# A spectral-mix kernel: six late weight steps become three, and half of their products become 48 small SBUF-to-SBUF transfers

## The chip, the cores and the metric

One core of one Trainium2 chip. The metric is device time in microseconds; the kernel before has a median of 180.15 us over 3 runs (179.83 to 180.81). The engines are called TensorE (matrix products, PE in the profile, its weight loads PEld), VectorE (DVE), ScalarE (ACT), GpSimd (POOL) and SyncE (SP). GpSimd and SyncE issue the transfers.

## The reference

`x` has 8 batches, 3264 positions and 192 channels. Two stages follow each other:

```python
w = softmax(weight)                        # 8 heads x 7 taps
x = causal_conv(x, w)                      # per head of 24 channels
X = rfft(x, axis=1)[:, :64]                # 64 modes, per batch and channel
Yr = Xr @ w_r - Xi @ w_i                   # per mode, 192 x 192
Yi = Xr @ w_i + Xi @ w_r
y = irfft(Y, n=3264)
u = x + y
out = u + maximum(u @ w_ch, 0)
```

All is linear up to the maximum, so `u @ w_ch` is computed as `x @ w_ch` plus the inverse transform of `Y @ w_ch`, and the output of a tile of 128 positions is the clamped sum of two products, plus the inverse transform of `Y`, plus `x`.

## The kernel before, in words

**Loads and convolution (to about 53 us).** GpSimd's queue loads `x` in units (L142) into `xall`, converted to bf16. TensorE convolves with banded matrices in `band` (L270), VectorE and ScalarE copy the result back over `xall` (L279, L277), and products with the cosine and sine table `ftab` (L288) give the spectrum, which `xtrans` lays out as `xt`, in the tile `mixa`.

**Mode products (about 68 to 108 us).** `mix(g, bank)` (L407) takes the 64 modes in 16 groups of four. The weights of a group are two transfers of 288 KB on GpSimd's queue (L251), 16 groups in all. The result of a group is a PSUM block whose partition is 32 x (mode within the group) + 8 x (real or imaginary) + batch; `mix_copy` (L420) copies it to `ymix`, two buffers used in turn. `mix_trans` (L424) transposes it on TensorE, and VectorE and ScalarE sort it into `yet` (L435, L437), with the channel as partition and batch, real or imaginary part and mode as columns. Between groups, transposes of `xall` into `ct` fill the time (`c_bank`, L381). For the last four groups that filling is used up, and `warm` (L533, its products are L536) puts filler products between: 12, 3, 5, 2 and 13.

**First weights.** For a batch `b`, `zw_mm` (L478) multiplies `yet` with `wm` and `w1`, which hold `w_ch` in columns 0 to 191 and an identity in columns 192 to 383. So one bank gets `Y @ w_ch` (used as "g") and `Y` back with modes as partitions ("y"), each 192 columns. `zw_out` (L482) scales it by `ascale` (1/S for mode 0, 2/S for the others) and writes it to `zw`, which lies over `xt` in `mixa`. Batches 0 and 1 are done ahead of the loop (L567 to L571).

**The output loop (about 109 to 174 us).** Two batches form a pair `q` (four pairs); two neighbouring tiles of positions form a duo (13 for each pair, 52 in all). Duos 0 and 1 are written out by hand with whole 128-row products (`full`, L522; `whole`, L573). The other 100 items, `(duo, a)` from duo 2 on, run through the loop at L635. TensorE works on the upper and lower 64 rows at once: for item k the lower rows' c and g products, for item k-2 the upper ones (L595), then a clamp by ScalarE (L514), then the y products of items k-4 and k-5. VectorE adds `x` to the bank (L501) and SyncE sends a duo out (L509). Eight PSUM banks go round in a ring (`next_of_ring`, L586), and seven output buffers in `arena`.

The order is written out by hand. `WEIGHTS` (L608) says after which loop steps the weights of batches 2 to 7 are made: six steps (9, 19, 29, 39, 51, 63), each with two products of 384 columns (L479, L480), a bank of the ring and a ScalarE scaling (L487). Pair 1 is first used by the g product of item 22 and by the y product of that item four steps later; pair 2 by item 48, pair 3 by item 74. Transfers on GpSimd's queue use eight completion counters in turn: a transfer waits for the one that was issued eight before it.

Of the kernel before, what the change touches and what calls it, by code (L numbers as in the profile page):

```python
# [9 lines left out]
ALU = mybir.AluOpType  # L10
ACT = mybir.ActivationFunctionType
AX = mybir.AxisListType
F32 = mybir.dt.float32
BF16 = mybir.dt.bfloat16
# [5 lines left out]
def kernel(  # L20
# [9 lines left out]
    nc = tc.nc  # L30
    B, S, D = x.shape
    H, KK = weight.shape
    MODES = moe_w_r.shape[0]
# [3 lines left out]
    P = 128  # L37
# [17 lines left out]
    def sb(name, shape, dtype):  # L55
        return pool.tile([P] + shape, dtype, tag=name, name=name)
# [8 lines left out]
    yet = sb("yet", [2, B, 2 * MODES], BF16)  # L65
    mixa = sb("mixa", [3 * 2 * B * MODES], BF16)
    xt = mixa[:, :].rearrange("p (j k m) -> p j k m", j=3, k=2 * B)
    zw = mixa[:, 0:2 * B * D].rearrange("p (t b d) -> p t b d", t=2, b=B)
    band = sb("band", [H, 2 * P], BF16)
    wm = sb("wm", [2 * D], BF16)  # L70
    w1 = sb("w1", [2 * D], BF16)
    wsw = sb("wsw", [2 * D], BF16)
# [2 lines left out]
    ascale = sb("ascale", [1], F32)  # L75
    halfpi = sb("halfpi", [1], F32)
    xs = [sb(f"xs{i}", [2, D], BF16) for i in range(2)]
    ymix = [sb(f"ymix{i}", [2, D], BF16) for i in range(2)]

    late = ct[:, 3 * NT * (NQ - 1):3 * NT * NQ, :].rearrange("p t s -> p (t s)")  # L80
    spots = [arena[:, WGB * i:WGB * (i + 1)] for i in range(NW)]
# [9 lines left out]
    def temp(n, dtype):  # L91
        w = n * 2 if dtype == F32 else n
        a = arena[:, pos[0]:pos[0] + w]
        pos[0] += (w + 15) // 16 * 16
        return a.bitcast(dtype) if dtype != BF16 else a

    turns = temp(NT * MODES, F32)
    whole = temp(NT * MODES, F32)
# [63 lines left out]
    nc.vector.memset(xall[HALF:P, NT:NSLOT:NT, :, :], 0.0)  # L162
    nc.vector.memset(halfpi[:], math.pi / 2)
    nc.vector.memset(ascale[:], 2.0 / S)
    nc.vector.memset(ascale[0:1, :], 1.0 / S)
    nc.vector.memset(ascale[64:65, :], 1.0 / S)
    for _ in range(NIDLE):
        nc.tensor.matmul(ZC[2][:, 0, 0:2 * D], xall[:, 0, 0, 0:P], xall[:, 0, :, :], start=True, stop=True,
                         skip_group_check=True)
    nc.vector.tensor_scalar(out=cidx[:, 0:PW], in0=cidx[:, 0:PW], scalar1=goff[:, 0:1], scalar2=None, op0=ALU.add)  # L170
    for k in range(KK):
        nc.vector.tensor_scalar(out=masks[:, PW * k:PW * (k + 1)], in0=cidx[:, 0:PW],
                                scalar1=float(KK - 1 - k), scalar2=None, op0=ALU.is_equal)
# [16 lines left out]
    for g in range(4):  # L190
        dst, srcv = band[32 * g:32 * g + 32, :, 32 * g:32 * g + PW], pk3[32 * g:32 * g + 32, :, :]
# [162 lines left out]
    ze, zm = [z[:, 0, :] for z in z4[0:2]], [z[:, 0, :] for z in z4[2:4]]  # L354
# [17 lines left out]
    def trans(o, in_):  # L372
        nc.tensor.matmul(o, in_, ident[:], start=True, stop=True, is_transpose=True)  # L373
# [33 lines left out]
    def mix(g, bank):  # L407
        yp = bank[:, D * (g % 2):D * (g % 2) + D]
        for j in range(3):
            for p4 in range(4):  # L410
                m = 4 * g + p4
                nc.tensor.matmul(yp[32 * p4:32 * p4 + 2 * B, :], xt[:, j, :, m],  # L412
                                 wts[g][:, p4, j, :], start=(j == 0), stop=(j == 2),
                                 tile_position=(0, 32 * p4), skip_group_check=True)
        if g < NW:
            load_w(g + NW + 3)
        elif g >= NW + 3:
            load_w(g + NW)

    def mix_copy(d, bank, g0, n):  # L420
        nc.scalar.copy(out=ymix[d % 2][:, g0:g0 + n, :],  # L421
                       in_=bank[:, D * g0:D * (g0 + n)].rearrange("p (g d) -> p g d", g=n))

    def mix_trans(d, g0, n):  # L424
        et = [z.bitcast(BF16)[:, 0:n * P].rearrange("p (g k) -> p g k", g=n) for z in ze]
        for t in range(2):
            for g in range(n):
                trans(et[t][:, g, :], ymix[d % 2][:, g0 + g, 64 * t:64 * t + P])
        m0 = 8 * d + 4 * g0
        for t in range(2):  # L430
            dst = yet[:, t, :, :].rearrange("p b (c m) -> p c b m", c=2)[:, :, :, m0:m0 + 4 * n]
            srcv = et[t].rearrange("p g (q k) -> p (g q) k", q=4)[:, :, 0:16].rearrange(
                "p m (c b) -> p c b m", c=2)
            if t == 0:
                nc.vector.tensor_copy(out=dst, in_=srcv)  # L435
            else:
                nc.scalar.copy(out=dst, in_=srcv)  # L437
# [15 lines left out]
    def turn(names):  # L453
        nop = nc.tensor.nop()
        for name in names:
            tc.add_manual_dep(nop.ins, name, mybir.DependencyInfo(mybir.DependencyClass.Sync,
                                                                  mybir.DependencyReason.DATA),
                              reason="row tiles take turns on a bank")
# [16 lines left out]
                last[row] = mm.ins.name  # L475
        held[n] = (first, last)

    def zw_mm(b, bank):  # L478
        nc.tensor.matmul(bank[:, 0:2 * D], yet[:, 0, b, :], wm[:], start=True, stop=False)  # L479
        nc.tensor.matmul(bank[:, 0:2 * D], yet[:, 1, b, :], w1[:], start=False, stop=True)  # L480

    def zw_out(b, bank, on_scalar, t=None):  # L482
        ts = slice(0, 2) if t is None else slice(t, t + 1)
        dst = zw[:, ts, b, :]
        srcv = bank[:, 0:2 * D].rearrange("p (t d) -> p t d", t=2)[:, ts, :]
        if on_scalar:
            nc.scalar.activation(out=dst, in_=srcv, func=ACT.Copy, scale=ascale[:, 0:1])  # L487
        else:
            nc.vector.tensor_scalar(out=dst, in0=srcv, scalar1=ascale[:, 0:1], scalar2=None, op0=ALU.mult)

    duos = [((q, 2 * b), (q, 2 * b + 1)) for q in range(NQ) for b in range(NB)]
    N = len(duos)
    place = {}
# [17 lines left out]
    def clamp(bank, on_scalar=True):  # L511
        z = bank[:, 0:2 * D]
        if on_scalar:
            nc.scalar.activation(out=z, in_=z, func=ACT.Relu)  # L514
        else:
            nc.vector.tensor_scalar(out=z, in0=z, scalar1=0.0, scalar2=None, op0=ALU.max)
# [5 lines left out]
    def full(n, which, a):  # L522
        (q, t), _ = duos[n]
        nc.tensor.matmul(place[n][a][:, 0:2 * D], ftab[:, t + a, :],  # L524
                         zw[:, 0 if which == "g" else 1, 2 * q:2 * q + 2, :].rearrange("p b d -> p (b d)"),
                         start=False, stop=(which == "y"), skip_group_check=True)
# [6 lines left out]
    def warm(bank, n):  # L533

        for _ in range(n):
            nc.tensor.matmul(bank[:, 0:2 * D], xall[:, 0, 0, 0:P], xall[:, 0, :, :], start=True, stop=True,  # L536
                             skip_group_check=True)
# [11 lines left out]
    c_products(1)  # L549
    d = ND - 2  # L550
    mix(2 * d, zm[0])
    warm(zm[1], 12)
    mix(2 * d + 1, zm[0])
    mix_copy(d, zm[0], 0, 2)
    warm(zm[1], 3)
    mix_trans(d, 0, 2)
    warm(zm[1], 5)
    d = ND - 1
# [1 line left out]
    mix_copy(d, zm[1], 0, 1)  # L560
    warm(zm[0], 2)
    mix_trans(d, 0, 1)
    warm(zm[0], 13)
    mix(NG - 1, zm[0])
    mix_copy(d, zm[0], 1, 1)
    mix_trans(d, 1, 1)
    zw_mm(0, zm[0])  # L567
    zw_mm(1, zm[1])
    for t in range(2):
        zw_out(0, zm[0], False, t)  # L570
        zw_out(1, zm[1], True, t)  # L571

    def whole(n, which):  # L573
        for a in range(2):
            full(n, which, a)
# [10 lines left out]
    def next_of_ring():  # L586
        taken[0] += 1
        return ring[(taken[0] - 1) % 8]

    bank = {}  # L590
    end = {}

    def product(k, row, piece, first, last):
        cols, l, r = piece
        mm = nc.tensor.matmul(bank[k][:, cols], l, r, start=first, stop=last, skip_group_check=True)  # L595
        end[k, row] = mm.ins.name

    def pieces(k, row, which):
        if not 0 <= k < K:
            return []  # L600
        n, a = items[k]
        return [p for w in which for p in z_pieces(duos[n][a], row, w)]

    def take(k):
        bank[k] = next_of_ring()
        place.setdefault(items[k][0], []).append(bank[k])

    WEIGHTS = {9: 2, 19: 3, 29: 4, 39: 5, 51: 6, 63: 7}  # L608

    def upper_y(k):  # L610
        if 0 <= k < K - 2:
            turn([end[k, 0]])
            product(k, 1, pieces(k, 1, "y")[0], False, True)
            add(bank[k], *items[k])
# [10 lines left out]
    for k in range(LAG):  # L625
        take(k)
        for j, p in enumerate(pieces(k, 0, "c")):
            product(k, 0, p, j == 0, False)
    whole(0, "g")
    clamp(place[0][0], False)  # L630
    clamp(place[0][1])
    whole(1, "g")
    clamp(place[1][0], False)
    clamp(place[1][1])
    for k in range(K + 4):  # L635
        if LAG <= k < K:
            take(k)
        lower, upper = pieces(k, 0, "cg"), pieces(k - LAG, 1, "cg")
        if upper:
            turn([end[k - LAG, 0]])  # L640
        for j in range(4):
            if j == 2:
                upper_y(k - 5)
            if j == 3:
                lower_y(k - 4)
            if lower and (k >= LAG or j == 3):
                product(k, 0, lower[j], j == 0, False)
            if upper:
                product(k - LAG, 1, upper[j], False, False)
        if upper:  # L650
            clamp(bank[k - LAG])
        if k in WEIGHTS:
            z = next_of_ring()
            zw_mm(WEIGHTS[k], z)
            zw_out(WEIGHTS[k], z, True)
        if k in (1, 2):
            whole(k - 1, "y")
            for a in range(2):
                add(place[k - 1][a], k - 1, a)
# [32 lines left out]
```

## Time and profile before

| | |
|---|---|
| median of 3 runs | 180.15 us (179.83 to 180.81) |
| profiled execution | 180.46 us |
| its span in the profile | 178.0 us |
| busy: PE, DVE, ACT, POOL | 164.2, 120.2, 107.9, 49.5 us |
| L595, all products of the loop: 64x384 / 64x192 | 57.0 us (396) / 84.6 us (600) |
| L501, adds by VectorE | 57.1 us (104), 557 ns each |
| L514, clamps by ScalarE | 48.4 us (102), 475 ns each |
| L487, scalings by ScalarE in the loop | 575 ns each (6) |
| L509, transfers out | 54, 3.1 us to landing (median) |
| L251, weight transfers on GpSimd's queue | 32, 612 ns each to issue, 11.5 us to landing |

The span is what the profiler recorded between the first and the last instruction; the executions' times hold some microseconds more. A row of a view names an engine, a line of the kernel and an operation. "Idle before" is how long the engine had nothing to run, and the arrow names what ended that. The chain that ended last goes back from the last instruction to whatever released it, and prints it in order of time: start, length, what. Products of TensorE are pipelined, so one product's duration (323 ns for 384 columns) is longer than the distance between two (160 ns).

### The profile page before, as it was taken

How to read it: one execution, taken by the hardware profiler on the slowest of the kernel's cores; microseconds unless marked ns; L12 is line 12 of the kernel's file. 1: busy time of each engine (PE TensorE's matmuls, PEld its weight loads, DVE VectorE, ACT ScalarE, POOL GpSimd, SP SyncE). 2: the span in 40 equal slices, each digit the busy share in tenths (PEclk: the TensorE clock that was granted, in tenths of full speed). 3: DMA queues.
4: the chain of work that ended last, by engine and by line, in shares of the span. 5: the costliest groups of instructions: out<-in, count | busy, mean ns of one | idle time of the engine just before them, and what ended most of it. 6: DMA issues, size and time to landing. Idle time of an engine off the chain costs nothing.

```text
span 178.0 us, 6536 instructions
## 1 busy us (share of the span) xinstructions
PE 164.2 (92%) x2773; PEld 136.6 (77%) x2773; DVE 120.2 (68%) x224; ACT 107.9 (61%) x193; POOL 49.5 (28%) x78
## 2 busy tenths in 40 slices
PE   7977999999999988999697988999999999999990
PEld 3557989999899976899695543877787887899960
DVE  6669874365354644788764004888988988999991
ACT  6347784344534424877474114688788888888870
POOL 7998931555233244443442000000000000000000
PEclk9999999999999999999999999999999999999998
DMA  4999999999999999999999940588888979899996
GB/s 47 160 187 192 194 190 192 193 190 192 193 192 195 207 207 206 206 206 206 206 207 206 206 71 4 182 301 312 290 317 308 340 277 344 304 337 330 332 357 211
DMA packets 50029, 40.04 MB, mean 225 GB/s; under 512 B 28304, under 2 KB 50000, under 8 KB 50000
## 3 DMA queue, kind: packets, MB, share of 16 engines
q0 software_dynamic: 35488, 19.54, 79.3%
q1 hardware_dynamic: 14512, 20.09, 30.8%
q8 instruction: 21, 0.34, 0.8%
q14 instruction: 8, 0.07, 0.1%
HBM read 39.10 MB, written 20.05 MB: 332 GB/s over the span
## 4 chain that ended last, share of the span: by engine, by line
PE 54%; DMA 33%; POOL 6%; issue 2%; ACT 1%; DVE 0%; DVEq 0%; POOLq 0%
PE z L595 33%; DMA arena<-in_moe_w_i_dram 20%; PE z L270 10%; DMA ct<-in_moe_w_i_dram 6%; DMA xall<-in_x_dram 6%; PE z L288 5%; POOL xall L142 4%; PE z L536 1%; PE z L479 1%; PE z L524 1%; PE z L480 1%; POOL xall L230 1%; PE z L412 0%; ACT xall L277 0%; POOL arena L251 0%
## 5 line engine op out<-in xcount | busy, mean ns | idle before, releaser
L501 DVE TENSOR_TENSOR arena<-z,xall 128x384 f32<-128x384 f32 (+1 forms) x104 | 57.1, 557 | 6.1 <-PE z L595 4.0
L595 PE MATMUL z<-mixa,ftab 64*128 64x384 bf16 x396 | 57.0, 323 | 0.0
L514 ACT ACTIVATE z<-z 128x384 f32<-128x384 f32 x102 | 48.4, 475 | 11.8 <-PE z L595 3.0
L595 PEld LDWEIGHTS <-ct 64*128 64x128 bf16 x600 | 37.8, 94 | 8.1 <-PE z L595 1.9
L270 PE MATMUL z<-xall,band 128*64 128x192 bf16 (+3 forms) x832 | 39.0, 246 | 2.3 <-ACT band L193 1.1
L270 PEld LDWEIGHTS <-band 128*64 128x64 bf16 x832 | 36.3, 110 | 4.5 <-issue 2.3
L279 DVE CAST xall<-z 128x768 bf16<-128x768 f32 (+3 forms) x26 | 24.8, 956 | 22.0 <-PE z L270 19.6
L595 PE MATMUL z<-wsw,ct 64*128 64x192 bf16 x300 | 33.4, 242 | 0.0
L595 PEld LDWEIGHTS <-ftab 64*128 64x128 bf16 x396 | 32.2, 94 | 1.1 <-issue 0.3
L277 ACT CAST xall<-z 128x768 bf16<-128x768 f32 (+3 forms) x26 | 20.7, 798 | 20.1 <-PE z L270 19.9
L142 POOL DMA_DIRECT2D xall<-in_x_dram x26 | 23.6, 914 | 12.1 <-DMA xall<-in_x_dram 11.3
L595 PE MATMUL z<-wm,ct 64*128 64x192 bf16 x200 | 26.9, 244 | 0.0
L595 PE MATMUL z<-w,ct 64*128 64x192 bf16 x100 | 24.3, 243 | 0.0
L365 DVE COPY ct<-z 128x1024 bf16<-128x1024 bf16 x26 | 17.1, 687 | 7.7 <-PE z L373 4.8
L288 PE MATMUL z<-xall,ftab 128*64 128x384 bf16 (+1 forms) x208 | 21.0, 326 | 0.7 <-ACT xall L277 0.7
L373 PE MATMUL z<-ident,xall 128*128 128x128 bf16 x312 | 19.3, 219 | 0.2 <-ACT ftab L363 0.2
L373 PEld LDWEIGHTS <-xall 128*128 128x128 bf16 x312 | 17.7, 98 | 1.0 <-issue 0.3
L363 ACT COPY ct<-z 128x1024 bf16<-128x1024 bf16 x13 | 13.2, 1013 | 4.0 <-PE z L373 3.9
L288 PEld LDWEIGHTS <-ftab 128*64 128x64 bf16 (+1 forms) x208 | 13.5, 110 | 2.3 <-DVE xall L279 0.5
L251 POOL DMA_DIRECT2D arena<-in_moe_w_r_dram x13 | 8.0, 614 | 15.3 <-PE z L373 5.3
L421 ACT CAST ymix<-z 128x384 bf16<-128x384 f32 (+1 forms) x9 | 4.0, 444 | 13.1 <-PE z L412 13.0
L251 POOL DMA_DIRECT2D arena<-in_moe_w_i_dram x13 | 8.0, 613 | 11.3 <-DMA xall<-in_x_dram 5.5
(95 smaller groups left out, 122.5 us busy)
## 6 DMA issues: line engine op xcount, KB each, us to landing
out_dram<-arena SPq DMA_DIRECT2D x47, 384.0 KB, 3.2
xall<-in_x_dram POOLq DMA_DIRECT2D x14, 384.0 KB, 13.4
arena<-in_moe_w_r_dram POOLq DMA_DIRECT2D x13, 288.0 KB, 11.6
arena<-in_moe_w_i_dram POOLq DMA_DIRECT2D x13, 288.0 KB, 11.8
xall<-in_x_dram POOLq DMA_DIRECT2D x6, 432.0 KB, 13.8
ct<-in_moe_w_r_dram POOLq DMA_DIRECT2D x3, 288.0 KB, 11.2
ct<-in_moe_w_i_dram POOLq DMA_DIRECT2D x3, 288.0 KB, 11.2
out_dram<-arena SPq DMA_DIRECT2D x3, 288.0 KB, 3.4
```

The lines of the kernel that those rows point to most:

```text
L142: nc.gpsimd.dma_start(out=xall[:, s0:s0 + nf, i, :], in_=src)
L251: nc.gpsimd.dma_start(out=wts[g][64 * half:64 * half + 64, :, :, :], in_=src[4 * g:4 * g + 4, :, :].rearrange("m (p j) e -> p m j e", j=3))
L270: nc.tensor.matmul(o, lhs, xall[:, r0:r0 + 2 * n - 1:2, :, dsl], start=(main and a == 0), stop=not main, tile_position=(0, 64 * half), ski ...
L277: nc.scalar.copy(out=dst, in_=srcv)
L279: nc.vector.tensor_copy(out=dst, in_=srcv)
L288: nc.tensor.matmul(xp[r, :], ftab[0:k, t, r], xall[0:k, NT * q + t, :, :], start=(t == 0), stop=(t == NT - 1), tile_position=(0, 64 * hh), ...
L363: nc.scalar.copy(out=out, in_=in_)
L365: nc.vector.tensor_copy(out=out, in_=in_)
L373: nc.tensor.matmul(o, in_, ident[:], start=True, stop=True, is_transpose=True)
L501: nc.vector.tensor_tensor(out=o[0:pn, :, a, :], in0=bank[0:pn, 0:2 * D].rearrange("p (i d) -> p i d", i=2), in1=xall[0:pn, s + a, :, :], o ...
L514: nc.scalar.activation(out=z, in_=z, func=ACT.Relu)
L595: mm = nc.tensor.matmul(bank[k][:, cols], l, r, start=first, stop=last, skip_group_check=True)
```

## The change

`ymix` becomes one buffer for all 16 groups; it lies in a tile `shared` that also holds `band`, which is not used any more by then. The scaling moves from `zw_out` to `mix_copy`, so `Y` in `ymix` is final. `spread_y`, right after the last copy, moves `Y` of batches 2 to 7 to its places in `zw` by 48 transfers on GpSimd's queue: 6 batches x 4 modes of a group x (real, imaginary), each from one partition (16 groups of 192 elements) to 16 partitions. `zw_mm` makes one half, g or y. For batches 0 and 1 both halves are still made by products, g first; for the later pairs a loop step makes g of both batches of a pair in one bank, four products of 192 columns, after steps 14, 38 and 62. Duo 0's g products and clamps now stand ahead of the c products of item 1. Two of the filler counts go from 12 to 9 and from 13 to 10.

```diff
-    band = sb("band", [H, 2 * P], BF16)
+    shared = sb("shared", [MODES // 4 * D], BF16)
+    band = shared[:, 0:H * 2 * P].rearrange("p (h c) -> p h c", h=H)
+    ymix = shared[:, :].rearrange("p (g d) -> p g d", d=D)
-    ymix = [sb(f"ymix{i}", [2, D], BF16) for i in range(2)]
...
-    nc.vector.memset(ascale[0:1, :], 1.0 / S)
-    nc.vector.memset(ascale[64:65, :], 1.0 / S)
+    nc.vector.memset(ascale[0:2 * B, :], 1.0 / S)
...
     def mix_copy(d, bank, g0, n):
-        nc.scalar.copy(out=ymix[d % 2][:, g0:g0 + n, :],
-                       in_=bank[:, D * g0:D * (g0 + n)].rearrange("p (g d) -> p g d", g=n))
+        g = 2 * d + g0
+        srcv = bank[:, D * g0:D * (g0 + n)].rearrange("p (g d) -> p g d", g=n)
+        if g == 0:
+            nc.scalar.activation(out=ymix[:, 0, :], in_=srcv[:, 0, :], func=ACT.Copy, scale=ascale[:, 0:1])
+            g, n, srcv = 1, n - 1, srcv[:, 1:n, :]
+        nc.scalar.activation(out=ymix[:, g:g + n, :], in_=srcv, func=ACT.Copy, scale=2.0 / S)
+    def spread_y():
+        for b in range(2, B):
+            for p4 in range(4):
+                for c in range(2):
+                    r = 32 * p4 + B * c + b
+                    nc.gpsimd.dma_start(out=zw[64 * c + p4:64 * c + 64:4, 1, b, :], in_=ymix[r:r + 1, :, :])
...
+    def zw_mm(b, o, t):
+        cols = slice(D * t, D * t + D)
+        nc.tensor.matmul(o, yet[:, 0, b, :], wm[:, cols], start=True, stop=False, skip_group_check=True)
+        nc.tensor.matmul(o, yet[:, 1, b, :], w1[:, cols], start=False, stop=True, skip_group_check=True)
+    def zw_pair(q, bank):
+        for i in range(2):
+            zw_mm(2 * q + i, bank[:, D * i:D * i + D], 0)
+        nc.scalar.copy(out=zw[:, 0, 2 * q:2 * q + 2, :].rearrange("p b d -> p (b d)"), in_=bank[:, 0:2 * D])
...
     mix(2 * d, zm[0])
-    warm(zm[1], 12)
+    warm(zm[1], 9)
     mix(2 * d + 1, zm[0])
...
     mix_trans(d, 0, 1)
-    warm(zm[0], 13)
+    warm(zm[0], 10)
     mix(NG - 1, zm[0])
     mix_copy(d, zm[0], 1, 1)
     mix_trans(d, 1, 1)
-    zw_mm(0, zm[0])
-    zw_mm(1, zm[1])
-    for t in range(2):
-        zw_out(0, zm[0], False, t)
-        zw_out(1, zm[1], True, t)
+    spread_y()
+    for b in range(2):
+        zw_mm(b, zm[b][:, 0:D], 0)
+    for b in range(2):
+        zw_mm(b, ze[1][:, D * b:D * b + D], 1)
+    nc.vector.tensor_copy(out=zw[:, 0, 0, :], in_=zm[0][:, 0:D])
+    nc.scalar.copy(out=zw[:, 0, 1, :], in_=zm[1][:, 0:D])
+    nc.vector.tensor_copy(out=zw[:, 1, 0:2, :].rearrange("p b d -> p (b d)"), in_=ze[1][:, 0:2 * D])
...
-    WEIGHTS = {9: 2, 19: 3, 29: 4, 39: 5, 51: 6, 63: 7}
+    WEIGHTS = {14: 1, 38: 2, 62: 3}
...
         for j, p in enumerate(pieces(k, 0, "c")):
             product(k, 0, p, j == 0, False)
-    whole(0, "g")
-    clamp(place[0][0], False)
-    clamp(place[0][1])
-    whole(1, "g")
-    clamp(place[1][0], False)
-    clamp(place[1][1])
+        whole(k, "g")
+        clamp(place[k][0], False)
+        clamp(place[k][1])
...
         if k in WEIGHTS:
-            z = next_of_ring()
-            zw_mm(WEIGHTS[k], z)
-            zw_out(WEIGHTS[k], z, True)
+            zw_pair(WEIGHTS[k], next_of_ring())
```

More of the change, by code (lines that the diff above doesn't have):

```diff
@@ L427, in mix_trans @@
             for g in range(n):
-                trans(et[t][:, g, :], ymix[d % 2][:, g0 + g, 64 * t:64 * t + P])
+                trans(et[t][:, g, :], ymix[:, 2 * d + g0 + g, 64 * t:64 * t + P])
         m0 = 8 * d + 4 * g0
@@ L476, in both @@
         held[n] = (first, last)
[L478 to L489, printed above, removed]
+    def zw_mm(b, o, t):
[6 more added lines that the diff above has]
+        nc.scalar.copy(out=zw[:, 0, 2 * q:2 * q + 2, :].rearrange("p b d -> p (b d)"), in_=bank[:, 0:2 * D])
     duos = [((q, 2 * b), (q, 2 * b + 1)) for q in range(NQ) for b in range(NB)]
```

## Prediction

> **What bounds the kernel now.** I read the chain of work that ended last first, in order of time, because it splits the kernel into stages. Until 53 us it is loads of x and the convolution; from 55.02 to 103.43 us it is four waits for weight transfers (20.4% plus 6.3% of the span); from there to the end it is TensorE. The tail of that view:
>
> ```profile
> 104.70 2.11 PE z L536 x13
> 106.81 0.41 PE z L412 x11
> 107.22 0.02 issue
> 107.25 0.33 ACT ymix L421
> ...
> 109.00 0.60 PE z L595 x6
> 109.59 0.76 PE z L524 x4
> ...
> 116.10 0.27 PE z L479
> 116.37 0.16 PE z L480
> 116.54 5.85 PE z L595 x100
> 122.39 0.27 PE z L479
> 122.66 0.16 PE z L480
> 122.82 5.91 PE z L595 x100
> ```
>
> See two things. The last mode group's products (L412) follow 13 filler matmuls (L536) without a gap, so the filler stands on the path. And each weight step (L479, L480) stands on the path, 0.43 us of its own rows. Then the timeline of VectorE, which adds every tile (L501):
>
> ```profile
> 117.01 5.73 DVE L501 TENSOR_TENSOR arena<-z,xall 128x384 f32<-128x384 f32 x10 [0.65 <-PE z L595]
> 123.29 5.79 DVE L501 TENSOR_TENSOR arena<-z,xall 128x384 f32<-128x384 f32 x10 [0.55 <-PE z L595]
> 129.63 5.79 DVE L501 TENSOR_TENSOR arena<-z,xall 128x384 f32<-128x384 f32 x10 [0.55 <-PE z L595]
> ```
>
> Ten adds run almost back to back (one is 558 ns, their starts are 573 apart), then VectorE waits 0.55 us for TensorE, at each weight step and hardly elsewhere. So TensorE and VectorE are nearly level inside the loop, and a weight step costs both. The DMA rows of the page show what the new transfers must share:
>
> ```profile
> q0 software_dynamic: 35488, 19.54, 79.3%
> q1 hardware_dynamic: 14512, 20.09, 30.8%
> ...
> out_dram<-arena SPq DMA_DIRECT2D x47, 384.0 KB, 3.2
> ```
>
> GpSimd issues its last transfer at 94.8 us and is idle after; the output transfers land in 3.2 us (2.0 to 4.6) with the DMA engines 0.84 to 0.93 busy.
>
> **The change, part by part.** Profiled run: 180.46 us, span 178.0 (2.46 around it), 0.31 above the median of the three runs, 180.15. I sum differences and take them off the median.
>
> *Weight steps, six to three.* An old step is 2 products of 384 columns, issued 0.16 us apart; a new one is 4 of 192, which in L595 issue 0.08 apart in one row: 0.32 us either way, plus the same change between 64-row and 128-row products. So a step stays about 0.54 (starts of adds 1.11 apart across a step, less 0.573; the chain's own rows give 0.43 and VectorE's idle time 4.0 us in 7 waits, 0.57). Three fewer: -1.62 (-1.29 to -1.71). Three scalings of 575 ns leave ScalarE too, and three banks are no longer taken from the ring; ScalarE is busy 5.2 of 6.3 us per ten items, so nothing is counted.
>
> *Filler 13 to 10 before the last group.* Three times 0.162 (2.11/13) is 0.49. But that group's weights land at 106.3 in the trace (the last completion mark of its transfer), and its products start at 106.74, so at most 0.4 is free: -0.38 (0 to -0.41). Filler 12 to 9: the product behind it (100.64) starts when its weights land (100.6), and the next waits for a transfer until 103.47: 0.
>
> *First weights and the order after them.* Eight products of 192 columns for four of 384 (0.64 us both), but those of the first half come first, so the copies that L524 waits for start about 0.16 earlier, and one of six conversions is merged. The g products of duo 0 no longer wait behind all six c products (0.60). Now they start at 109.59; the copies would allow 0.3 less. -0.30 (0 to -0.5); TensorE is what is late next there.
>
> *48 transfers on GpSimd's queue.* Each moves 6 KB from one partition to 16. Not shown before; nearest rows: 0.56 us for 64 or 128 runs (wm, w), 0.61 for the weight loads, 0.91 for L142 with 1024 runs. I take 0.61: few runs, and the same back-to-back queue. They wait for the last spectrum copy (107.57, with the gain 107.2) and start at 107.3; behind them on GpSimd is nothing but one another. Landing: I take 4.6, the longest output transfer. TensorE first needs Y of pair 1 in loop step 26, pair 2 in 52, pair 3 in 78; counted from the chain that is 126.7, 143.3 and 158.8 now, 125.5, 141.0 and 156.5 with the gains. The transfers arrive at 107.3 + 16 x 0.61 + 4.6 = 121.7, then 131.4 and 141.2. Cover 3.8, 9.6 and 15.3 us: cost 0. At 0.91 each, pair 1 is 1.0 late: +1.0. The free price is 0.85 us; below nothing there is no gain, since nothing they replace is on the path except the steps above.
>
> The Trainium skill (SBUF — State Buffer, Who interferes with whom) says that GpSimd cannot write descriptors while VectorE runs an operation that holds their common port, and gives 3100 ns for a transfer that takes 620 alone. Here the weight loads took 612 to 642 ns whether or not VectorE was copying banks (L365), but none was issued beside L501. By 3100 ns the 48 would end 149 us after 107.3, and the sum would be some 100 us worse.
>
> *New waits.* The weight loads of the first y products of each later pair wait for four transfer counters each, the products for one more. In the trace L412's first weight load has two extra semaphore instructions, 51 ns for the one already satisfied. Six loads with three extras each: 0 to +0.9, I take +0.45, half hidden under running products. Everything of TensorE, and so VectorE's adds, queues behind these.
>
> *DMA engines.* 768 packets at about 63 ns (79.3% of 16 x 178 us over 35488) are 3.0 us of all 16 engines, spread over 29 us where they are busy up to 0.91. Output transfers could land later; seven output buffers (8 us of adds) hide that: 0 (to +1.0). The rest (one longer pair of copies for group 0 at 69.7 us, one memset of 59 ns less) lies in stretches that wait for transfers: 0.
>
> Sum: -1.62 -0.38 -0.30 +0.45 = -1.85: 178.61 for the profiled run, **178.3** against the median. Bounds: -1.71 -0.41 -0.5 = 177.5, and -1.29 +0.9 +1.0 = 180.8.
>
> **Rivals.**
> 1. *GpSimd is held up by VectorE's adds* (slower). From 112 us an add fills 558 of every 573 ns. If each transfer has to wait for one add to end, it costs 0.56 + 0.61 = 1.17. Eight are out by 112.2; the other 40 take 46.8, landing at 163.6 against 156.5: 7.1 late, **185.4**. It makes the kernel slower than before from 1.04 us a transfer on. For: no row shows the pair side by side. Against: copies beside the weight loads did nothing. The Trainium skill (SBUF — State Buffer, Who interferes with whom) also speaks against it: a VectorE operation with at most one input in SBUF, outside its two-port modes, does not take the common port; no run here shows it.
> 2. *Landing is the limit.* Eight counters serve the queue, so transfer n+8 waits for n. At the weight loads' 11.5 us, six rounds of eight take 69 us, 176.3 against 156.5: **198**. It decides from 6.8 us a landing. Against: 8 x 288 KB at the 206 GB/s of that stage is 11.4 us, so 11.5 is the queue's own backlog; these carry 6 KB.
> 3. *The steps were not what paced the loop:* VectorE or the output traffic takes the time back. VectorE alone needs 104 x 0.573 = 59.6 us; from 110.5 that ends at 170.1, before the 171.9 forecast for its last add. If it did, only filler and start-up remain, less the waits: 180.15 - 0.68 + 0.45 = **179.9**. For: VectorE is 97% busy from 160 us. Against: its idle gaps stand at the steps.
>
> That the change does not do what it says is excluded by the built order: 48 transfers and three steps stand in it.
>
> The Trainium skill (DMA: Bandwidth & Descriptors, Anatomy of one DMA) gives about 2.0 us fixed per transfer, so 96 us for 48 one after another, some 47 us later than needed. The trace has weight loads issued 0.63 us apart (85.39, 86.02) that land over 10 us later, so fixed times overlap; by the rule the sum holds only because of that.
>
> **How the numbers follow.** Forecast 0.65; rival 1 0.11; rival 2 0.05; rival 3 0.13; a transfer price of 0.85 to 1.0, which eats part or all of the gain, 0.06. A measurement tells about 0.5% from no change: 179.25 to 181.05. Of the forecast a little reaches into that band, and of the last case a little leaves it on the slow side: faster 0.67, same 0.15, slower 0.18. The range, 177.4 to 180.8, takes in the bounds and rival 3, and leaves out rivals 1 and 2.
>
> **What would show it.** Three L479-like pairs instead of six in the chain; VectorE waits at steps 14, 38 and 62 only; filler of 10 followed by the last group near 106.4; transfers at about 0.61 us ending near 137; no wait of TensorE for a transfer after 107 us. I am wrong if such a wait appears at the first y products of a pair, if the spread passes 0.85 us per transfer, or if VectorE's adds are no longer 573 ns apart.

## The result, and the profile after

The changed kernel has a median of 178.69 us (177.4 to 179.89, 20 runs), the kernel before 180.22 us (179.05 to 183.87, 20 runs). The ratio is 0.992, with a 95% interval of 0.990 to 0.995: faster by 0.8%, some 1.4 us. The forecast was 178.3 us, faster, with a range of 177.4 to 180.8.

The profiled execution took 179.81 us and its span is 177.8, only 0.2 less than before. That execution's loads came late: the weights of the last mode group landed at 108.02 us instead of 106.3. Over all profiles here the group ahead of the last starts anywhere from 103.2 to 105.2 us, whatever the kernel. So I compare from there on, in three lengths: the gap between the products of the last two groups, from the last group to VectorE's first add, and from the first add to the end of the last one.

TensorE's timeline ahead of the loop, before and then after:

```profile
103.47 0.46 PE L412 MATMUL z<-arena,mixa 128*16 128x192 bf16 x12 [0.52 <-DMA arena<-in_moe_w_i_dram]
...
104.53 2.28 PE L536 MATMUL z<-xall 128*128 128x384 bf16 x13
106.74 0.46 PE L412 MATMUL z<-arena,mixa 128*16 128x192 bf16 x12
```

```profile
105.17 0.46 PE L413 MATMUL z<-arena,mixa 128*16 128x192 bf16 x12 [0.56 <-DMA arena<-in_moe_w_i_dram]
...
106.19 1.79 PE L548 MATMUL z<-xall 128*128 128x384 bf16 x10
108.07 0.46 PE L413 MATMUL z<-arena,mixa 128*16 128x192 bf16 x12
```

The group ahead of the last starts at 105.17, the last 2.90 us later, and now the ten filler products (L548, L536 before) end first: the chain of work has a transfer ending at 108.02 ahead of it, and the group's first weight load stands idle for 0.48 us until then (0.32 before, with no transfer at its end). Before, the gap was 3.27 and filler filled it. The chain from there on:

```profile
110.27 0.08 PE z L496
110.35 0.35 PE z L610 x3
110.70 0.43 PE z L536 x2
111.13 0.35 PE z L610 x3
111.48 0.43 PE z L536 x2
...
120.53 0.19 PE z L495
120.72 0.08 PE z L496
120.80 0.08 PE z L495
120.88 0.08 PE z L496
120.97 13.93 PE z L610 x215
```

L610 and L536 are here what L595 and L524 were. Two things are to be seen. Three c products, two g products, three and two take 1.56 us; before, six and four took 1.36. And a weight step is 0.43 us of its own rows, as an old one was. VectorE's first and last rows of adds before (L501), and then all of them after (L513):

```profile
111.08 1.97 DVE L501 TENSOR_TENSOR arena<-z,xall 128x384 f32<-128x384 f32 x4 [0.15 <-PE z L524]
...
151.00 23.20 DVE L501 TENSOR_TENSOR arena<-z,xall 128x384 f32<-128x384 f32 x41 [0.61 <-PE z L595]
```

```profile
112.64 1.97 DVE L513 TENSOR_TENSOR arena<-z,xall 128x384 f32<-128x384 f32 x4 [0.29 <-PE z L536]
115.07 5.71 DVE L513 TENSOR_TENSOR arena<-z,xall 128x384 f32<-128x384 f32 x10 [0.46 <-PE z L610]
121.44 13.75 DVE L513 TENSOR_TENSOR arena<-z,xall 128x384 f32<-128x384 f32 x24 [0.65 <-PE z L610]
135.80 13.78 DVE L513 TENSOR_TENSOR arena<-z,xall 128x384 f32<-128x384 f32 x24 [0.61 <-PE z L610]
150.21 23.77 DVE L513 TENSOR_TENSOR arena<-z,xall 128x384 f32<-128x384 f32 x42 [0.62 <-PE z L610]
```

VectorE runs 24 and 42 adds without a wait, their starts still 573 ns apart (24 in 13.75 us). From 115.07 on it waits for TensorE at the three steps only. From the first add at 112.64 to the end at 150.21 + 23.77 is 61.34 us; before it was 63.12 (111.08 to 151.00 + 23.20). The new transfers, by their line:

```profile
L436 POOL DMA_DIRECT2D mixa<-shared x48: 483/483/519, 109.2 to 133.9; - x48
...
DMA to landing us min/median/max: 1.6/3.5/5.1
```

Shortest, median and longest issue are 483, 483 and 519 ns, with adds running beside most of them. The last issue ends at 134.4 us; the waits of pair 3's first products stand at about 158. The chain holds no wait for a transfer after 108.02.

### The profile page after: what moved, and what is told of

It reads as the page before. It is cut to its first block, busy times and chain, and to the rows that moved or that the text cites. A ratio compares the mean times of both kernels' runs of the same rounds, so it can differ in the third digit from the quotient of the medians.

```text
span 177.8 us, 6583 instructions
## 1 busy us (share of the span) xinstructions
PE 162.0 (91%) x2771; PEld 139.0 (78%) x2771; DVE 121.1 (68%) x223; ACT 106.1 (60%) x190; POOL 72.2 (41%) x126
## 4 chain that ended last, share of the span: by engine, by line
DMA 56%; PE 36%; POOL 3%; issue 2%; DVE 0%; DVEq 0%; ACT 0%; POOLq 0%
PE z L610 33%; DMA xall<-in_x_dram 30%; DMA arena<-in_moe_w_i_dram 20%; DMA ct<-in_moe_w_i_dram 6%; POOL xall L144 2%; PE z L536 1%; PE z L495 1%; PE z L496 0%; DVE arena L513 0%; PE z L413 0%; DVEq L697 0%; ACT shared L428 0%; POOL arena L153 0%; PE z L374 0%; DVE yet L449 0%
## 5 line engine op out<-in xcount | busy, mean ns | idle before, releaser
L513 DVE TENSOR_TENSOR arena<-z,xall 128x384 f32<-128x384 f32 (+1 forms) x104 | 57.5, 557 | 4.1 <-PE z L610 2.3
L610 PE MATMUL z<-mixa,ftab 64*128 64x384 bf16 x396 | 57.4, 322 | 0.0
L610 PEld LDWEIGHTS <-ct 64*128 64x128 bf16 x600 | 39.3, 94 | 4.6 <-issue 0.9
L271 PE MATMUL z<-xall,shared 128*64 128x192 bf16 (+3 forms) x832 | 39.2, 246 | 3.7 <-DMA xall<-in_x_dram 1.6
L271 PEld LDWEIGHTS <-shared 128*64 128x64 bf16 x832 | 36.5, 110 | 5.7 <-issue 3.0
L610 PE MATMUL z<-wsw,ct 64*128 64x192 bf16 x300 | 36.6, 243 | 0.0
L610 PEld LDWEIGHTS <-ftab 64*128 64x128 bf16 x396 | 29.8, 94 | 0.9 <-issue 0.3
L610 PE MATMUL z<-wm,ct 64*128 64x192 bf16 x200 | 29.1, 243 | 0.0
L436 POOL DMA_DIRECT2D mixa<-shared x48 | 22.9, 487 | 14.8 <-ACT shared L428 12.5
L610 PE MATMUL z<-w,ct 64*128 64x192 bf16 x100 | 24.3, 243 | 0.0
```

Source lines behind the costliest of these rows:

```text
L271: nc.tensor.matmul(o, lhs, xall[:, r0:r0 + 2 * n - 1:2, :, dsl], start=(main and a == 0), stop=not main, tile_position=(0, 64 * half), ski ...
L436: nc.gpsimd.dma_start(out=zw[64 * c + p4:64 * c + 64:4, 1, b, :], in_=ymix[r:r + 1, :, :])
L513: nc.vector.tensor_tensor(out=o[0:pn, :, a, :], in0=bank[0:pn, 0:2 * D].rearrange("p (i d) -> p i d", i=2), in1=xall[0:pn, s + a, :, :], o ...
```

## The experiments

All lengths in us, from each run's profile. The ratio is to the kernel before, timed on the same chip, with its interval; that kernel's median was 180.70 beside e1 to e4, 180.74 beside e5 to e7 and 180.08 beside e8 and e9, so medians of different groups of runs are not compared directly. The expectations of e1 to e3 end the third length 0.47 us earlier, at 173.51, where the chain's row of the last add ends: their 60.87 for the changed kernel is the 61.34 of this table. A few tenths of a microsecond are below what the ratios can tell, but the three lengths repeat within 0.05 between profiles of the same kernel.

| run | gap of the last two groups | last group to first add | first add to end of last | median | ratio |
|---|---|---|---|---|---|
| before | 3.27 | 4.34 | 63.12 | 180.22 | 1 |
| changed kernel | 2.90 | 4.57 | 61.34 | 178.69 | 0.992 (0.990 to 0.995) |
| e1_old_filler | 3.23 | 4.58 | 61.29 | 179.47 | 0.994 (0.990 to 0.997) |
| e2_old_order | 2.90 | 4.37 | 61.29 | 178.38 | 0.989 (0.984 to 0.994) |
| e3_six_short | 2.88 | 4.57 | 61.95 | 179.25 | 0.993 (0.990 to 0.996) |
| e4_96_transfers | 2.89 | 4.58 | 66.92 | 184.25 | 1.021 (1.017 to 1.026) |
| e5_before_filler | 2.88 | 4.34 | 63.12 | 180.00 | 0.995 (0.992 to 0.997) |
| e6_two_early | 2.88 | 5.03 | 61.95 | 179.97 | 0.996 (0.992 to 0.999) |
| e7_six_wide | 2.89 | 4.58 | 62.90 | 180.25 | 0.998 (0.995 to 1.002) |
| e8_changed_again | 2.89 | 4.58 | 61.29 | 178.46 | 0.991 (0.988 to 0.995) |
| e9_old_order_again | 2.87 | 4.38 | 61.33 | 178.47 | 0.988 (0.984 to 0.992) |

### The filler: e1 and e5

```diff
 e1, on the changed kernel          e5, on the kernel before
-    warm(zm[1], 9)                 -    warm(zm[1], 12)
+    warm(zm[1], 12)                +    warm(zm[1], 9)
...
-    warm(zm[0], 10)                -    warm(zm[0], 13)
+    warm(zm[0], 13)                +    warm(zm[0], 10)
```

> The changed kernel with the old filler counts, 12 and 13. Theory: with 10 filler products the last mode group starts when its weights land (2.90 us after the group ahead of it); with 13 it starts when the filler ends, 3.27 after, so this run has 0.37 more there and the same from the first add to the end of the last (60.87 us): total 0.4 us above the changed kernel. Rival: the weights land late anyway in most executions, so that filler paces nothing: gap 2.9, total unchanged.

> The kernel before with the new filler counts alone, 9 and 10. Theory: from the start of the products of the last mode group but one to those of the last, 3.27 us become 2.9, then set by the weights' landing; the 4.34 us to the first add and the 63.1 from there to the end of the last add stay: 0.35 us less in all. Rival: the weights land later than the filler ends in most executions, gap unchanged, 0.

The gap goes from 2.90 to 3.23 in e1 and from 3.27 to 2.88 in e5, and the other two lengths stay. e5, in TensorE's timeline (L412 is the mode product, L536 the filler):

```profile
105.18 0.46 PE L412 MATMUL z<-arena,mixa 128*16 128x192 bf16 x12 [0.53 <-DMA arena<-in_moe_w_i_dram]
...
106.24 1.79 PE L536 MATMUL z<-xall 128*128 128x384 bf16 x10
108.06 0.46 PE L412 MATMUL z<-arena,mixa 128*16 128x192 bf16 x12
```

So three filler products less ahead of the last group are worth 0.33 to 0.39 us, on either kernel; the rival, that the weights land too late for it to matter, falls. The median of e5 fell by more, its ratio leaving 0.9 us (0.5 to 1.4). The profile has no second place for it, and what of that is more than the spread of the load stage stays open.

### The order ahead of the loop: e2 and e9

```diff
     for b in range(2):
-        zw_mm(b, ze[1][:, D * b:D * b + D], 1)
-    nc.vector.tensor_copy(out=zw[:, 0, 0, :], in_=zm[0][:, 0:D])
-    nc.scalar.copy(out=zw[:, 0, 1, :], in_=zm[1][:, 0:D])
-    nc.vector.tensor_copy(out=zw[:, 1, 0:2, :].rearrange("p b d -> p (b d)"), in_=ze[1][:, 0:2 * D])
+        zw_mm(b, zm[b][:, D:2 * D], 1)
+    for t in range(2):
+        nc.vector.tensor_copy(out=zw[:, t, 0, :], in_=zm[0][:, D * t:D * t + D])
+        nc.scalar.copy(out=zw[:, t, 1, :], in_=zm[1][:, D * t:D * t + D])
...
             product(k, 0, p, j == 0, False)
+    for k in range(LAG):
         whole(k, "g")
```

> The changed kernel with the order of before around the first weights: all six c products of items 0 and 1, then the g products of duos 0 and 1, and the y halves in the upper columns of the banks of the g halves. Theory: the alternation of 64-row and 128-row products costs TensorE two more changes, so the way from the last group's products to the first add falls from 4.57 us back to about 4.34, or 0.1 less since the g copies start earlier. Rival: the longer way comes from VectorE's merged copy of 0.56 us ahead of its first clamp; splitting it then gives as much, and the two are told apart by which engine the first g and y products wait for. From the first add to the last: 60.9 either way.

> The run with the order of before around the first weights once more, now beside the changed kernel. Theory: 4.37 and 61.3, so 0.2 us (0.1%) below the changed kernel, less than an interval of five rounds tells apart; the stage's times in the profile tell it. Rival: the 0.3 us between their medians of the first call is more than the 0.2 of the stage, so something else gains as well: below 0.997 of the changed kernel here.

The middle length falls from 4.57 to 4.37 and 4.38. The chain of e2 at that place:

```profile
109.00 0.60 PE z L610 x6
109.60 0.76 PE z L536 x4
110.36 0.43 PE z L610 x2
```

These are the lengths of the kernel before, 1.36 us, instead of 0.35, 0.43, 0.35 and 0.43. What is saved, 0.2 us, is TensorE's own: the two changes between 64-row and 128-row products that the alternation adds. The rows of e2 and of the changed kernel give the price of one: six and three c products take 0.60 and 0.35, so 0.083 each and 0.10 on top, and four and two g products take 0.76 and 0.43, so 0.165 each and again 0.10 on top. e2 splits VectorE's merged copy as well, but in both versions the chain stays on TensorE there, so that copy is not what paces it. In medians the two versions cannot be told apart (178.46 and 178.47 side by side in e8 and e9), so the 0.3 us between their first medians was spread.

> The changed kernel once more, beside the next run on the same chip. Theory: from the last group to the first add 4.57, from there to the end of the last add 61.3; 0.992 of the kernel before, as measured. Rival: the 0.8% was of that chip, 1.0 here.

The changed kernel came out at 0.991, and the lengths repeat; the rival, 1.0, falls.

### What a weight step costs: e3 and e7

e3 keeps the 12 narrow products and spreads them over six steps. e7 keeps the transfers, but has the six steps of before, with a y half that nothing uses.

```diff
-    WEIGHTS = {14: 1, 38: 2, 62: 3}
+    WEIGHTS = {9: 2, 19: 3, 29: 4, 39: 5, 51: 6, 63: 7}
...
 e3
-            zw_pair(WEIGHTS[k], next_of_ring())
+            z, b = next_of_ring(), WEIGHTS[k]
+            zw_mm(b, z[:, 0:D], 0)
+            nc.scalar.copy(out=zw[:, 0, b, :], in_=z[:, 0:D])
...
 e7
-            zw_pair(WEIGHTS[k], next_of_ring())
+            z, b = next_of_ring(), WEIGHTS[k]
+            nc.tensor.matmul(z[:, 0:2 * D], yet[:, 0, b, :], wm[:], start=True, stop=False)
+            nc.tensor.matmul(z[:, 0:2 * D], yet[:, 1, b, :], w1[:], start=False, stop=True)
+            nc.scalar.copy(out=zw[:, 0, b, :], in_=z[:, 0:D])
```

> The changed kernel with six weight steps of two products of 192 columns (one batch each, after steps 9, 19, 29, 39, 51 and 63) instead of three of four. The same 12 products, three more steps. Theory: a step is 0.32 us of products plus about 0.28 for the change between 64-row and 128-row products and back, so three more changes: 60.87 plus 0.84 is 61.7 from the first add to the last, VectorE waiting about 0.44 at each of six steps. Rival: only the columns count, 60.9.

> The changed kernel with the transfers and their waits, but with the six wide weight steps of before (two products of 384 columns each, y half computed and not used; a copy of 192 columns instead of a scaling of 384). So the loop has the work of before and the transfers on top. Theory: transfers and waits are hidden, the whole gain of the loop is the steps: 63.1 us from the first add to the end of the last, as in the kernel before (63.12). Rival: the transfers (DMA engines, 12 extra semaphore instructions) cost the loop 0.3 to 1.0: 63.4 to 64.1, and the steps are worth so much more than was measured.

VectorE's waits in e3 and in e7, of two steps each:

```profile
124.00 5.73 DVE L513 TENSOR_TENSOR arena<-z,xall 128x384 f32<-128x384 f32 x10 [0.39 <-PE z L610]
130.18 5.73 DVE L513 TENSOR_TENSOR arena<-z,xall 128x384 f32<-128x384 f32 x10 [0.44 <-PE z L610]
```

```profile
123.14 5.73 DVE L513 TENSOR_TENSOR arena<-z,xall 128x384 f32<-128x384 f32 x10 [0.55 <-PE z L610]
129.47 5.73 DVE L513 TENSOR_TENSOR arena<-z,xall 128x384 f32<-128x384 f32 x10 [0.60 <-PE z L610]
```

Over all steps, one of two wide products costs VectorE 0.55 to 0.65 (e7, 0.58 on average), one of two narrow products 0.39 to 0.49 (e3), one of four narrow products 0.61 to 0.65 (changed kernel, 0.63 on average); in each version the first step is the dearest. The loop (first add to end of last) reads 62.90 in e7, 61.95 in e3 and 61.34 in the changed kernel. So half the columns give 0.95 us (e7 to e3; twelve products at 0.08 less are 0.96), and three steps fewer with the same products another 0.61, 0.20 each. Neither theory of e3 had the size: steps count, but 0.6 in all and not 0.84. Three steps fewer are also three banks of the ring and three ScalarE copies fewer, which e3 does not separate; but two changes at 0.10 each, from the rows of e2, make the same 0.20. The Trainium skill (TensorEngine Tiling (Array Packing), Key Properties) says that changing the tiling mode drains TensorE. The 0.20 for going to 128-row products and back agrees with that; no run here shows the drain itself.

e7 has the loop work of before plus the transfers, and its loop is 62.90 against 63.12: the transfers and their waits cost the loop nothing that shows. It is even 0.22 shorter. Most runs of ten adds last 5.73 there and 5.79 in the kernel before; e7's ScalarE copies take 318 ns where the old scaling of twice the width took 575. That the shorter copy is the cause was not tried by itself, so a small cost of the transfers beside a larger gain of the copy is not excluded.

### When the transfers stop being free: e4

```diff
-                    nc.gpsimd.dma_start(out=zw[64 * c + p4:64 * c + 64:4, 1, b, :], in_=ymix[r:r + 1, :, :])
+                    for h in range(2):
+                        lo = 64 * c + 32 * h + p4
+                        nc.gpsimd.dma_start(out=zw[lo:64 * c + 32 * h + 32:4, 1, b, :], in_=ymix[r:r + 1, 8 * h:8 * h + 8, :])
```

> The changed kernel with each of the 48 transfers cut into two of 8 partitions: 96, the same bytes. Theory: the transfers are free only as long as GpSimd's queue is ahead of the loop. At 0.48 to 0.50 us each from 109.2 us on, pair 1 is complete at 128.7 with 3.5 of landing against 127.6 needed, pair 2 at 144.7 against 143.1, pair 3 at 160.7 against 158.0: TensorE waits for transfers at the first y products of each pair, 2.7 us in all (1 to 5), and the kernel loses what the change gained. Rival: with half the packets each transfer is cheaper, or the seven output buffers take the wait up: 0 to +0.5.

GpSimd's line (L438), VectorE's adds (L515) and the end of the chain in e4:

```profile
L438 POOL DMA_DIRECT2D mixa<-shared x96: 497/499/538, 107.9 to 158.6; - x96
```

```profile
127.63 6.86 DVE L515 TENSOR_TENSOR arena<-z,xall 128x384 f32<-128x384 f32 x12 [0.62 <-PE z L612]
...
145.73 5.71 DVE L515 TENSOR_TENSOR arena<-z,xall 128x384 f32<-128x384 f32 x10 [2.65 <-PE z L612]
152.02 9.16 DVE L515 TENSOR_TENSOR arena<-z,xall 128x384 f32<-128x384 f32 x16 [0.58 <-PE z L612]
163.67 14.59 DVE L515 TENSOR_TENSOR arena<-z,xall 128x384 f32<-128x384 f32 x26 [2.49 <-PE z L612]
```

```profile
158.64 4.54 DMA mixa<-shared
163.18 0.14 issue
163.31 13.44 PE z L612 x177
```

Half the bytes cost the same issue, 499 ns instead of 483. With the waits for the eighth transfer before (3.8 us in all) a transfer takes 0.53 us on average, and 96 of them end at 159.2. Adds that ran through in the changed kernel now stop for 0.62, 2.65 and 2.49 us, at pairs 1, 2 and 3 (the row between is a weight step), and the loop is 5.6 us longer: the kernel is slower than before by 2%. The view of L438 has TensorE's weight loads wait for these transfers three times, 4.3 us in all, and in the chain TensorE goes on at 163.31, when the last one has landed. The mechanism is the one that was expected, the size is above the 1 to 5 given. The average price was taken at 0.50 without the waits for counters, which is 3.3 us less over 96 transfers, and the last one took 4.5 us to land, not 3.5. Nothing gave the time back: the rival falls.

### Steps ahead of the loop: e6

```diff
 on e2
-    WEIGHTS = {14: 1, 38: 2, 62: 3}
+    WEIGHTS = {62: 3}
...
         clamp(place[k][1])
+    for q in (1, 2):
+        zw_pair(q, next_of_ring())
     for k in range(K + 4):
```

> The run with the old order, and the weight steps of pairs 1 and 2 moved ahead of the loop, right behind the g products of duo 1, which are 128-row products as well; pair 3 stays at step 62. Theory: there a step costs its products only, four of 0.08 to 0.11, partly beside the clamps that the first y products wait for; the loop loses two steps of 0.63. From the last group to the first add 4.4 to 5.1 (4.37 without), from the first add to the last 60.0 (61.29 without): 0.6 to 1.2 us less in all, the fastest version here. Rival: VectorE is level with TensorE by then (104 adds at 0.573 are 59.6) and the two more banks in the ring hold the loop: 60.5 or more, nothing gained in all.

The adds of e6:

```profile
112.15 1.02 DVE L513 TENSOR_TENSOR arena<-z,xall 128x384 f32<-128x384 f32 x2 [0.81 <-PE z L536]
113.66 1.02 DVE L513 TENSOR_TENSOR arena<-z,xall 128x384 f32<-128x384 f32 x2 [0.48 <-PE z L536]
115.27 0.56 DVE L513 TENSOR_TENSOR arena<-z,xall 128x384 f32<-128x384 f32 x1 [0.59 <-PE z L610]
116.49 0.56 DVE L513 TENSOR_TENSOR arena<-z,xall 128x384 f32<-128x384 f32 x1 [0.66 <-PE z L610]
117.65 32.06 DVE L513 TENSOR_TENSOR arena<-z,xall 128x384 f32<-128x384 f32 x56 [0.59 <-PE z L610]
```

The first of three such places in its chain:

```profile
112.12 0.03 issue
112.15 0.57 DVE arena L513
112.72 0.04 issue
112.76 0.59 PE z L610 x8
```

The two steps vanish from the loop, as meant (56 adds without a wait), but the way to the first add grows by 0.65 and VectorE waits five times at the start. The chain shows why: TensorE there waits for adds three times (1.3 us in all), because an add has to free a bank. By the program's order the two early steps take the ring's next banks, so items 2 and on get banks that duos 0 and 1 still hold. The loop comes to 61.95, and the version is 1.3 us behind e2 by the three lengths. My theory fell; the ring's part of the rival was right, by these waits. No run gave the early steps banks of their own.

## Why the prediction was right, point by point

The sum was -1.85; the lengths give -0.37 + 0.23 - 1.78 = -1.92 between the two profiles, and the medians -1.5. The mechanism was right where most of the gain lies, in the steps and the filler. That the total of the lengths came out within 0.1 is luck: the order after the first weights was 0.53 worse than forecast, and against it stand 0.45 of waits that cost nothing and 0.22 in the loop that were not counted.

- **Weight steps, -1.62:** right. e7 to the changed kernel is -1.56. The price per step was near level, as assumed: in VectorE's waits a narrow step of four is slightly dearer (0.63 on average) than a wide one of two (0.58); two more weight loads may be the reason, not tried alone.
- **Filler, -0.38:** right, -0.37 between the profiles, 0.33 and 0.39 in e1 and e5. That 12 to 9 gives nothing agrees: the two groups behind it wait for their transfers (0.84 and 0.56 us).
- **First weights and the order after them, -0.30 (0 to -0.5):** wrong in sign, +0.23. The step left out what the new order does to TensorE: two more changes between 64-row and 128-row products, 0.2 us (e2, e9). The g products do start 0.22 sooner after the last group (2.63 instead of 2.85), but the chain behind them is longer. VectorE's first copy does start 0.15 sooner after the last group (1.89 instead of 2.04), but the chain does not run through it. With the old order (e2) the first add comes 4.37 after the last group, so the changed kernel would be 0.2 us better with that order.
- **Transfers, cost 0 at 0.61 each:** right, with a price of 0.48 each, and 0.525 with the waits for counters. Landing has a median of 3.5, the 4.6 assumed is near the longest, 5.1. e7 has no cost in the loop that shows, and e4 shows that they do cost once the queue falls behind.
- **New waits, +0.45:** mis-sized. There are 12 extra semaphore instructions, not the 18 counted, 51 ns each in the median and 243 at most, and adds run through them (24 in 13.75 us): 0. What failed is the step that everything of TensorE queues behind these: VectorE shows no such wait.
- **DMA engines, 0:** right; landing of output transfers went from 3.2 to 3.7 us in the median, and no add is shown waiting for it.
- **ScalarE, not counted:** probably -0.2, by the comparison of e7 with the kernel before.
- **Rival 1** (GpSimd waits for adds, 1.17 us a transfer) falls: 483 ns with adds beside. By the Trainium skill (SBUF — State Buffer, Who interferes with whom) an operation of VectorE with at most one SBUF input, outside its two-port modes, does not contend with GpSimd. The trace agrees: an add has one input in PSUM and one in SBUF, and the shortest and the median issue are both 483 ns; the 3100 ns that the page gives for another operation did not occur. **Rival 2** (landing) falls: 5.1 us at most, below the 6.8 from which it decides. **Rival 3** (the steps do not pace the loop) falls: VectorE's waits went with the steps, and the loop became 1.78 us shorter.

## What to carry to other kernels

A side step in a loop where two engines are level costs both, and its price is the products plus the change of row mode around them; count the changes, also where an edit only reorders products. Small transfers on GpSimd's queue were priced here by the piece (0.5 us, with eight in flight), not by the byte (3 KB or 6 KB): they are free as long as the queue stays ahead of the first use, so work out the date of each use and compare. When moving steps to an idle place, check which buffers they hold there.

## What was not expected of the hardware

A transfer of 8 rows of 384 bytes took GpSimd 499 ns to issue, one of 16 rows 483: the smaller one is no cheaper. Going from 64-row products to 128-row products and back cost TensorE about 0.20 us. And the waits in front of weight loads, 51 ns each in the median, vanished under the running products.
